# Taking the sign into the slope of an activation while 64-bit weights are decoded, and a new emission order

## The chip, the cores and the metric

The kernel runs on one core of a Trainium2 chip. The metric is device time in microseconds of one execution, the median of several. The engines are named as in the profile: PE (TensorE), DVE (VectorE), ACT (ScalarE), POOL (GpSimd) and SP (SyncE, which here issues nearly all DMAs). Each runs its own queue in order, and they wait for each other by semaphores.

## The reference, cut to what matters

An mLSTM layer over 4 batches, 8 heads, 768 steps and 40 channels, then a gated feed-forward layer over the 3072 tokens of 320 channels.

```python
for t in range(S):
    m_new = np.maximum(f_gate[:, :, t] + m, i_gate[:, :, t])
    f_stab, i_stab = np.exp(f_gate[:, :, t] + m - m_new), np.exp(i_gate[:, :, t] - m_new)
    C = f_stab * C + i_stab * outer(v_t, k_t);  n = f_stab * n + i_stab * k_t
    y[:, :, t] = sigmoid(o_gate[:, :, t]) * (C @ q_t) / np.maximum(np.abs(n . q_t), 1.0)
x = y.transpose(0, 2, 1, 3).reshape(B * S, H * D)
out = (sigmoid(x @ w_gate) * (x @ w_val)) @ w_out
```

The three weights (320x1536 twice, 1536x320) arrive as 64-bit floats. No engine computes on those, so the kernel reads them as pairs of 32-bit words and makes the 32-bit float out of the bits.

## The kernel before, in words

The 768 steps are cut into 6 chunks of 128. A chunk c and a batch b make a *unit* u = 4c + b (8 heads of 128 steps), 24 units in all. A unit goes through stages: `a` transposes q and k and lays q out block-diagonally; `e` (`dmat`) makes the matrix of decays, an exponential and a mask; `b` makes the scores and multiplies them with the decays; `c` multiplies with v, adds what comes from the state, divides by the denominator (`halfden`, `times_den`), updates the state and issues the loads of the same batch's next chunk; `d` transposes the result into the feed-forward layer's input (`xh`, `xl`, a high and a low part, since PE's fast format holds fewer bits).

The feed-forward layer of a chunk has 12 steps j over the hidden channels. A *tile* is one step for some batches: (c, j, 0, 4) for all four, or two half tiles (c, j, 0, 2) and (c, j, 2, 4). PARAM['K'] says how many steps of a chunk are halved; for chunk 0 it is 4, so its tiles 0 to 7 are halves: tiles 0 to 3 for batches 0 and 1, tiles 4 to 7 for batches 2 and 3. Tiles 8 to 15 of chunk 0 are whole. `ffn_up` makes gate and value on PE (L496 to L501), a tanh on ACT (L503), the product on DVE (L504), the high part on ACT (L507) and the low part on DVE (L508). `ffn_down` adds to the four outputs (L518 to L520).

The weights are decoded on the way, all during chunk 0. There are 30 decodings, numbered in `wseq`: for each i of 6, gate rows, value rows, the rest rows of both, and two blocks of w_out. One decoding (`w_dec`) is: the absolute value of the high word on ACT (L242, into one of three buffers `dc`); a clamp (L247) and a mask with shift by 3 bits (L248) on DVE; an OR of the sign and the top bit of the exponent (L252) and an OR of the low word's top 3 bits (L253) on DVE; the high part on ACT (L278, L281 or L283); the low part on POOL (L288, L292 or L294), with which the buffer is free. `w_more` then issues the load of a later weight block on SP into the staging tile that came free.

The opening handles units 0 and 1 and decodings 0 to 2 in an order given by PARAM['open'] (names such as `wvb`: weight, value, stage b; `kw0`: k times the last decays, unit 0). All else is emitted in the order of PARAM['pos'], where position n is n whole tiles of feed-forward work after its start; a half tile takes half a position. In the text "before tile n" counts the tiles above, while positions count whole ones. Positions are first pushed to where the data need them. A down-projection of the tile before comes at PARAM['down'] of a tile. Work below PARAM['pin'] is held behind the opening on each engine, and `opening_end` (the states of units 0 and 1) comes at PARAM['ce']. The emission order decides the queues' order but for priorities: decodings have a raised one (WPO), stages too (HPO).

Of the kernel before, what the change touches and what calls it, by code (L numbers as in the profile page):

```python
# [9 lines left out]
F32 = mybir.dt.float32  # L10
F32R = mybir.dt.float32r
I32 = mybir.dt.int32
AF = mybir.ActivationFunctionType
ALU = mybir.AluOpType

EXP_LOW = struct.unpack("<f", struct.pack("<I", 0x38000000))[0]
EXP_HIGH = struct.unpack("<f", struct.pack("<I", 0x47EFFE00))[0]


PARAM = {  # L20
    'pos': {
# [15 lines left out]
    },  # L37
    'V32': 1,
    'HPO': 1,
    'WPO': 10,  # L40
    'TS': False,
    'down': 0.6,
    'K': [4, 12, 3, 0, 0, 12],
    'eng': {
# [3 lines left out]
    },  # L48
    'warm': 6,
    'pin': 2,  # L50
    'ce': -9,
    'open': {
# [8 lines left out]
        'wvc': 59.0, 'wvd': 60.0, 'na1': 69.87, 'xt0': 62.0, 'wve': 63.0, 'wrb': 64.0, 'nb1': 62.99, 'wrc': 61.877,  # L61
        'xt1': 56.016, 'wrd': 70.043, 'wre': 69.0, 'kw1': 70.0, 'e2': 87.0,
    },
    'unpin': [],
}
# [4 lines left out]
def mlstm_then_gated_ffn_kernel(  # L70
# [13 lines left out]
    nc = tc.nc  # L84
# [139 lines left out]
    wh, wl, w2 = [], [], []  # L224
# [14 lines left out]
    def decode_abs(st, n):  # L239
        dc = stage.tile([P, 2 * FW], F32, tag="dc", name=f"dc_{n}", bufs=3)  # L240
        t = dc[:, : st.shape[1]]
        nc.scalar.activation(t, st[:, :, 1].bitcast(F32), AF.Abs)  # L242
        return t

    def decode_exp(st, t):
        ti = t.bitcast(I32)
        nc.vector.tensor_scalar(t, t, EXP_LOW, EXP_HIGH, ALU.max, ALU.min)  # L247
        nc.vector.tensor_scalar(ti, ti, 0x07FFFFFF, 3, ALU.bitwise_and, ALU.logical_shift_left)  # L248

    def decode_bits(st, t):  # L250
        ti = t.bitcast(I32)
        nc.vector.scalar_tensor_tensor(ti, st[:, :, 1], -0x40000000, ti, ALU.bitwise_and, ALU.bitwise_or)  # L252
        nc.vector.scalar_tensor_tensor(ti, st[:, :, 0], 29, ti, ALU.logical_shift_right, ALU.bitwise_or)  # L253

    wq = {}
# [40 lines left out]
    def w_dec(part, i):  # L296
        st = w_stage(part, i)
        t = decode_abs(st, f"{part}_{i}")
        decode_exp(st, t)
        decode_bits(st, t)  # L300
        w_high(part, i, t)
        w_low(part, i, t)
# [235 lines left out]
    def opening():  # L538
# [130 lines left out]
        def w_a(x):  # L669
            w[x] = decode_abs(w_stage(*x), "%d_%d" % x)  # L670

        def w_b(x):
            decode_exp(w_stage(*x), w[x])

        def w_c(x):
            decode_bits(w_stage(*x), w[x])
# [169 lines left out]
    ce = PARAM["ce"]  # L846
    for p, (kind, kk) in events:
        if ce is not None and p >= ce:
            pinned(opening_end)
            ce = None  # L850
# [33 lines left out]
```

## Time and profile before

| | |
|---|---|
| median of 3 runs | 612.86 us (609.75 to 613.76) |
| the profiled execution | 612.63 us, span 610.9 us, mean granted clock 0.963 |
| busy in the span | PE 93%, DVE 65%, ACT 38%, POOL 36% |
| instructions | 9801 |
| moved by DMA | 43.91 MB, mean 72 GB/s |

The span runs from the first to the last instruction; the execution's time has some more around it. Busy times are of one execution. A row of a group gives line, engine, operation, output and inputs, count, busy us and mean ns; a row of the timeline gives start, duration, engine, line, and in brackets the idle time before it and what ended it; a row of stretches gives start:end, length, then busy time and count of PE, PEld (weight loads), DVE, ACT and POOL, the granted clock of PE as a share of full speed, the DMA share and GB/s.

### The profile page before, as it was taken

How to read it: one execution, taken by the hardware profiler on the slowest of the kernel's cores; microseconds unless marked ns; L12 is line 12 of the kernel's file. 1: busy time of each engine (PE TensorE's matmuls, PEld its weight loads, DVE VectorE, ACT ScalarE, POOL GpSimd, SP SyncE). 2: the span in 40 equal slices, each digit the busy share in tenths (PEclk: the TensorE clock that was granted, in tenths of full speed). 3: DMA queues.
4: the chain of work that ended last, by engine and by line, in shares of the span. 5: the costliest groups of instructions: out<-in, count | busy, mean ns of one | idle time of the engine just before them, and what ended most of it. 6: DMA issues, size and time to landing. Idle time of an engine off the chain costs nothing.

```text
span 610.9 us, 9801 instructions
## 1 busy us (share of the span) xinstructions
PE 566.9 (93%) x3601; PEld 511.4 (84%) x3601; DVE 396.4 (65%) x822; ACT 234.1 (38%) x580; POOL 221.6 (36%) x277
## 2 busy tenths in 40 slices
PE   8568898898999999999989999989999999999997
PEld 7456787676999899898878888879788888999997
DVE  5798889997454887846676647566656566533332
ACT  5274557535343334442332252332242322132322
POOL 5466355955142464524343324432322321100000
PEclk9766899998999999999999999998899999999999
DMA  9774665413132224413032232131232200010000
GB/s 194 227 180 130 128 187 147 125 33 88 45 78 68 73 50 115 92 28 79 12 77 58 56 76 64 25 77 37 43 79 54 57 1 0 1 45 1 23 1 21
DMA packets 112847, 43.91 MB, mean 72 GB/s; under 512 B 101280, under 2 KB 104544, under 8 KB 112800
## 3 DMA queue, kind: packets, MB, share of 16 engines
q1 hardware_dynamic: 111712, 43.04, 28.6%
q8 instruction: 28, 0.46, 0.3%
q10 hardware_dynamic: 1088, 0.26, 0.2%
q14 instruction: 19, 0.16, 0.1%
HBM read 39.26 MB, written 4.03 MB: 71 GB/s over the span
## 4 chain that ended last, share of the span: by engine, by line
PE 63%; DVE 20%; DMA 4%; ACT 3%; issue 3%; SPq 3%; POOL 3%; DVEq 0%; POOLq 0%; ACTq 0%
PE pg L496 25%; PE po L520 5%; PE po L519 5%; PE po L518 5%; PE av L416 5%; PE pg L498 4%; PE pg L501 4%; DVE bh L369 3%; PE s L400 3%; DVE gl L508 3%; PE in L411 2%; DVE dc L253 2%; DVE kl L362 2%; DVE dc L252 2%; DVE sg L504 1%
## 5 line engine op out<-in xcount | busy, mean ns | idle before, releaser
L496 PE MATMUL pg<-xh,wh 128*128 128x256 f32 (+1 forms) x412 | 118.9, 353 | 3.3 <-ACT sg L503 1.6
L504 DVE SCALAR_TENSOR_TENSOR sg<-sg,pg 128x256 f32<-128x256 f32 (+1 forms) x103 | 53.9, 523 | 100.5 <-ACT sg L503 93.7
L503 ACT ACTIVATE sg<-pg 128x256 f32<-128x256 f32 (+1 forms) x103 | 48.3, 469 | 182.7 <-PE pg L501 178.4
L496 PE MATMUL pg<-xh,wl 128*128 128x256 f32 (+1 forms) x412 | 113.9, 343 | 0.0
L496 PE MATMUL pg<-xl,wh 128*128 128x256 f32 (+1 forms) x412 | 110.1, 336 | 0.0
L520 PE MATMUL po<-oh,gl 128*128 128x320 f32 x288 | 97.1, 339 | 1.9 <-DVE gl L508 1.9
L519 PE MATMUL po<-ol,gh 128*128 128x320 f32 x288 | 97.1, 337 | 0.0
L518 PE MATMUL po<-oh,gh 128*128 128x320 f32 x288 | 94.9, 329 | 0.4 <-ACT gh L507 0.4
L508 DVE TENSOR_TENSOR gl<-sg,gh 128x256 fp32r<-128x256 f32 (+1 forms) x103 | 69.2, 672 | 30.4 <-ACT gh L507 29.2
L496 PEld LDWEIGHTS pg<-xh,wh 128*128 128x128 f32 x412 | 72.7, 194 | 10.9 <-DVE sg L504 2.7
L496 PEld LDWEIGHTS pg<-xh,wl 128*128 128x128 f32 x412 | 72.1, 195 | 6.5
L496 PEld LDWEIGHTS pg<-xl,wh 128*128 128x128 f32 x412 | 71.8, 194 | 6.5
L369 POOL TENSOR_TENSOR bl<-kl,bmask 120x384 fp32r<-120x384 f32 (+1 forms) x48 | 49.3, 1032 | 58.2 <-DVE kl L362 56.1
L507 ACT ACTIVATE gh<-sg 128x256 fp32r<-128x256 f32 (+1 forms) x103 | 51.6, 501 | 48.4 <-DVE sg L504 48.1
L520 PEld LDWEIGHTS po<-oh,gl 128*128 128x128 f32 x288 | 54.8, 191 | 4.3 <-DVE gl L508 4.0
L518 PEld LDWEIGHTS po<-oh,gh 128*128 128x128 f32 x288 | 55.5, 193 | 3.0 <-ACT gh L507 0.6
L519 PEld LDWEIGHTS po<-ol,gh 128*128 128x128 f32 x288 | 55.2, 191 | 0.8
L416 PEld LDWEIGHTS av<-v,d 128*128 128x128 f32 x352 | 52.0, 191 | 3.3 <-DVE d L393 2.2
L498 PE MATMUL pg<-xh,w 128*128 128x256 f32 (+1 forms) x206 | 53.5, 336 | 0.0
L501 PE MATMUL pg<-xl,w 128*128 128x256 f32 (+1 forms) x206 | 52.7, 333 | 0.0
L416 PE MATMUL av<-v,d 128*128 128x41 f32 x352 | 49.9, 254 | 2.1 <-DVE d L393 1.6
L218 POOL TENSOR_SCALAR_AFFINE_SELECT d<-d 128x1024 f32<-128x1024 f32 x22 | 26.8, 1220 | 66.2 <-ACT d L213 61.5
(132 smaller groups left out, 977.9 us busy)
## 6 DMA issues: line engine op xcount, KB each, us to landing
d<-mscr SPq DMA_DIRECT2D x22, 512.0 KB, 3.8
k<-in_k_dram SPq DMA_DIRECT2D x24, 160.0 KB, 3.4
v<-in_v_dram SPq DMA_DIRECT2D x24, 160.0 KB, 3.7
o<-in_o_gate_dram SPq DMA_DIRECT2D x24, 160.0 KB, 3.4
st_o<-in_moe_w_out_dram SPq DMA_DIRECT2D x12, 320.0 KB, 2.9
out_dram<-ob SPq DMA_DIRECT2D x24, 160.0 KB, 1.8
q<-in_q_dram SPq DMA_DIRECT2D x23, 160.0 KB, 2.9
st<-in_moe_w_gate_dram SPq DMA_DIRECT2D x6, 512.0 KB, 3.7
```

The costliest lines, as they stand in the source:

```text
L369: eng.tensor_tensor(dst[:r, g, :nh, :], src[:r, g, 0, :].bitcast(F32).unsqueeze(1).broadcast_to([r, nh, L]), bmask[:r, :nh, :], ALU.mult)
L416: nc.tensor.matmul(pv[:, h, :], dm[u][:, h, :], vt[u][:, h, :], start=True, stop=True)
L496: nc.tensor.matmul(pg[n], w[n][:, a, fs], x[c][:, a, n0:n1], start=(i + a == 0), stop=False)
L498: nc.tensor.matmul(pg[n], w2[n][:, fs], xh[c][:, 2, n0:n1], start=False, stop=False)
L501: nc.tensor.matmul(pg[n], w2[n][:, fs], xl[c][:, 2, n0:n1], start=False, stop=True)
L503: nc.scalar.activation(sg, pg[0], AF.Tanh, scale=0.5)
L504: nc.vector.scalar_tensor_tensor(sg, sg, 1.0, pg[1], ALU.add, ALU.mult)
L507: last = nc.scalar.activation(gh[u][:, :nt], sg, AF.Copy)
L508: E('gl0' if c == 0 else 'gl').tensor_tensor(gl[u][:, :nt], sg, gh[u][:, :nt].bitcast(F32), ALU.subtract)
L518: nc.tensor.matmul(po[t], g1[:, ts], oh[:, j, :], start=(j == 0), stop=False)
L519: nc.tensor.matmul(po[t], g1[:, ts], ol[:, j, :], start=False, stop=False)
L520: nc.tensor.matmul(po[t], g0[:, ts], oh[:, j, :], start=False, stop=(j == NF - 1))
```

## The change

The absolute value on ACT becomes a leaky slope: f(x) = x for x >= 0, alpha * x for x < 0, on x times 2^-112, with alpha = 2^32. A positive number comes out scaled by 2^-112, a negative one by 2^-80. The difference of 32 in the exponent puts the sign where the shift by 3 bits brings it to the top, with the exponent's top bit right for both signs. So the clamp gets other bounds, the mask before the shift goes, and the OR of the sign (L252) goes. The tiles, buffers and engines of what is left are the same.

Besides, nearly all positions of PARAM['pos'] and PARAM['open'] are new, with `down` 0.6 to 0.66, `pin` 2 to 4.6, `ce` -9 to -8.79.

```diff
-EXP_LOW = struct.unpack("<f", struct.pack("<I", 0x38000000))[0]
-EXP_HIGH = struct.unpack("<f", struct.pack("<I", 0x47EFFE00))[0]
+MAX_POS = struct.unpack("<f", struct.pack("<I", 0x0FEFFFFF))[0]
+MAX_NEG = struct.unpack("<f", struct.pack("<I", 0x9FEFFFFF))[0]
...
-    'down': 0.6,
+    'down': 0.66,
...
-    'pin': 2,
-    'ce': -9,
+    'pin': 4.6,
+    'ce': -8.79,
...
-        nc.scalar.activation(t, st[:, :, 1].bitcast(F32), AF.Abs)
+        nc.scalar.activation(t, st[:, :, 1].bitcast(F32), AF.Prelu, scale=2.0**-112, alpha=2.0**32)
...
-        nc.vector.tensor_scalar(t, t, EXP_LOW, EXP_HIGH, ALU.max, ALU.min)
-        nc.vector.tensor_scalar(ti, ti, 0x07FFFFFF, 3, ALU.bitwise_and, ALU.logical_shift_left)
+        nc.vector.tensor_scalar(t, t, MAX_POS, MAX_NEG, ALU.min, ALU.max)
+        nc.vector.tensor_scalar(ti, ti, 3, None, ALU.logical_shift_left)
...
-        nc.vector.scalar_tensor_tensor(ti, st[:, :, 1], -0x40000000, ti, ALU.bitwise_and, ALU.bitwise_or)
         nc.vector.scalar_tensor_tensor(ti, st[:, :, 0], 29, ti, ALU.logical_shift_right, ALU.bitwise_or)
```

Of the new positions, those of chunk 0 that stand elsewhere in the sorted order (p before -> after, in whole tiles):

| event | before | after |
|---|---|---|
| stages b, c, d of unit 2 | 1.01, 1.30, 1.42 | 0.70 |
| stages a, b, c, d of unit 3 | 1.01, 1.30, 1.30, 1.60 | 0.70 |
| first down-projection | 0.80 (at 0.6 of a tile of 0.5, from 0.5) | 0.83 |
| stages a, b, d of unit 4 | 2.18, 4.53, 5.50 | 1.79, 3.89, 7.62 |
| decodings 19; 20 to 22; 23; 24, 25 | 7.38; 7.99; 8.99; 9.99 | 7.38; 7.42; 7.44; 7.45 |
| decodings 26, 27 | 9.99 | 9.99 |
| stage e of units 7, 8 | 9.99, 12.73 | 11.32, 16.27 |

Later units see stage e moved by up to 1.7 later or 1.1 earlier, stages a and b by up to 2.1 earlier, stage c of the third batch by 1 later, and stage d of unit 10 by 2.2 later. In the opening `kw0` goes from behind `dl0` to behind `wvb`.

More of the change, by code (lines that the diff above doesn't have):

```diff
@@ L49 @@
     'warm': 6,
-    'pin': 2,
-    'ce': -9,
+    'pin': 4.6,
+    'ce': -8.79,
     'open': {
[8 rows of a table removed]
-        'wvc': 59.0, 'wvd': 60.0, 'na1': 69.87, 'xt0': 62.0, 'wve': 63.0, 'wrb': 64.0, 'nb1': 62.99, 'wrc': 61.877,
-        'xt1': 56.016, 'wrd': 70.043, 'wre': 69.0, 'kw1': 70.0, 'e2': 87.0,
[9 rows of a table added]
+        62.625, 'wve': 63.0, 'wrb': 63.947, 'nb1': 61.739, 'wrc': 61.877, 'xt1': 57.363, 'wrd': 70.043, 'wre': 69.0,
+        'kw1': 70.796, 'e2': 87.005,
     },
```

47 rows, old and new, of the table PARAM are left out of this document.

## The prediction, made before the result was known

> **What bounds the kernel now.** I read the shares of the engines first, then the busy time by stretches, then the cadence of the feed-forward tiles, then the chain that ended last.
>
> ```profile
> PE 566.9 (93%) x3601; PEld 511.4 (84%) x3601; DVE 396.4 (65%) x822; ACT 234.1 (38%) x580; POOL 221.6 (36%) x277
> ...
> 0.00:30.00 30.00, 20.96 (x114) 17.95 (x114) 18.91 (x41) 12.21 (x34) 14.42 (x35) 0.89 0.87 213
> 30.00:55.00 25.00, 17.01 (x71) 13.33 (x71) 24.97 (x61) 15.84 (x49) 17.55 (x17) 0.57 0.60 148
> 55.00:75.00 20.00, 18.14 (x113) 15.92 (x113) 15.18 (x37) 10.86 (x34) 8.50 (x13) 0.85 0.58 137
> 75.00:150.00 75.00, 66.17 (x370) 55.97 (x370) 68.32 (x125) 42.82 (x106) 48.18 (x47) 0.98 0.44 121
> 150.00:611.00 461.00, 444.61 (x2941) 408.23 (x2939) 269.05 (x562) 152.36 (x360) 132.91 (x168) 0.99 0.20 48
> ```
>
> Over the whole span TensorE is the bound, but the average hides two regimes. In the rows of the stretches (PE, PEld, DVE, ACT, POOL, then the granted clock) PE is busy 96% after 150 us and DVE only 58%. Between 30 and 55 us DVE is busy 24.97 of 25.00 us while PE has 17.01 at a granted clock of 0.57; between 75 and 150 us DVE has 91% and PE 88%. So VectorE sets the pace up to 150 us, TensorE after it. How much is to be had there? One tanh (L503) stands in each feed-forward tile:
>
> ```profile
> 39.10 0.38 ACT L503 ACTIVATE sg<-pg 128x256 f32<-128x256 f32 x1
> ...
> 77.70 0.38 ACT L503 ACTIVATE sg<-pg 128x256 f32<-128x256 f32 x1 [1.88 <-PE pg L501]
> ...
> 118.49 0.60 ACT L503 ACTIVATE sg<-pg 128x512 f32<-128x512 f32 x1
> 126.04 0.60 ACT L503 ACTIVATE sg<-pg 128x512 f32<-128x512 f32 x1 [2.12 <-PE pg L501]
> 138.10 0.60 ACT L503 ACTIVATE sg<-pg 128x512 f32<-128x512 f32 x1
> ...
> 156.08 0.38 ACT L503 ACTIVATE sg<-pg 128x256 f32<-128x256 f32 x1 [2.14 <-PE pg L501]
> ```
>
> The first chunk of 12 tiles runs from 39.10 to 156.08, 117.0 us; the other five share 610.9 - 156.1 = 454.8 us, 91.0 each. The first is 26 us slower, and 39.10 to 77.70 alone (two tiles, 38.6 us where 2 x 7.6 is the later pace) accounts for 23 of them. That is the room for any change to the decoding.
>
> **The removed OR.** L252 is the sign's OR, L253 the other one, which stays. The first two rows give min/median/max in ns; the next four are the busy time of L252 alone, by the same stretches.
>
> ```profile
> L252 DVE SCALAR_TENSOR_TENSOR dc<-st,dc x18: 410/683/1382, 6.7 to 134.8; 128x512 int32<-128x512 int32 x12, 128x256 int32<-128x256 int32 x6
> L252 DVE SCALAR_TENSOR_TENSOR dc<-st_o,dc x12: 472/482/2069, 37.4 to 146.3; 128x320 int32<-128x320 int32 x12
> ...
> 0.00:30.00 30.00, 1.79 (x3) 0.89 0.87 213
> 30.00:55.00 25.00, 4.11 (x6) 0.57 0.60 148
> 55.00:75.00 20.00, 1.16 (x2) 0.85 0.58 137
> 75.00:150.00 75.00, 15.47 (x19) 0.98 0.44 121
> ```
>
> Thirty instructions go: 22.5 us measured. Their unstretched price is 12 x 0.683 + 6 x 0.410 + 12 x 0.480 = 16.4 us. The difference of 6 us is waiting, and this is what such a wait looks like:
>
> ```profile
> 46.95 1.88 POOL L218 TENSOR_SCALAR_AFFINE_SELECT d<-d 128x1024 f32<-128x1024 f32 x1
> 47.19 0.68 DVE L252 SCALAR_TENSOR_TENSOR dc<-st,dc 128x512 int32<-128x512 int32 x1
> ...
> 47.99 1.38 DVE L253 SCALAR_TENSOR_TENSOR dc<-st,dc 128x512 int32<-128x512 int32 x1
> 49.29 0.28 DVE L247 TENSOR_SCALAR dc<-dc 128x256 f32<-128x256 f32 x1
> ```
>
> L253 takes twice its median while POOL's mask of 1.88 us runs, yet the L252 just before it is not stretched, so the stretch isn't strict. I expect it to pass to the next instruction when one is removed, and count 16.4; 22.5 stays as the upper end. The Trainium skill ("SBUF — State Buffer", section "SBUF: two separate sides") says more: GpSimd and a VectorE instruction with two SBUF inputs take a port pair by exclusive lock. By that rule the whole excess would move on, as I count it; the unstretched row at 47.19 does not agree with it.
>
> Stretch by stretch:
>
> *0 to 30 us.* Only the third OR stands before something that PE waits for:
>
> ```profile
> 25.08 0.42 DVE L252 SCALAR_TENSOR_TENSOR dc<-st,dc 128x256 int32<-128x256 int32 x1
> 25.54 0.42 DVE L253 SCALAR_TENSOR_TENSOR dc<-st,dc 128x256 int32<-128x256 int32 x1
> 25.89 0.16 DVE L431 TENSOR_SCALAR den<-av 128x8 f32<-128x8 f32 x1
> ...
> 27.78 1.20 PE L452 MATMUL xt<-ident,x 128*128 128x128 f32 x3 [4.62 <-POOL x L441]
> ```
>
> The denominator of the second unit stands behind it, POOL's product behind that, PE's transposition last. Start to start the OR takes 25.54 - 25.08 = 0.46 us: I count 0.4. The other two (1.4 us) lie beside the waits for PE and ACT: nothing.
>
> *30 to 75 us.* DVE never rests until 55, so all six ORs there are on the path: unstretched 3 x 0.48 + 2 x 0.683 + 0.41 = 3.2. Of the two after it (1.16), half: 0.6. Bounds 2.2 (what of them the chain holds, below) and 5.3.
>
> *75 to 150 us.* Nineteen ORs, 15.5 us measured, unstretched 8 x 0.48 + 7 x 0.683 + 4 x 0.41 = 10.3. The chain gives the lower end:
>
> ```profile
> by line: DMA v<-in_v_dram 16.9%; DMA q<-in_q_dram 12.7%; DVE dc L252 9.5%; PE pg L496 8.2%; DVE dc L253 8.2%; issue 7.2%; DVE gl L508 4.6%; DVE qbd L346 4.1%; DVE gin L168 3.1%; ACT d L209 3.1%; PE po L520 3.0%; PE s L392 2.8%; DVE dc L247
> by line: DVE gl L508 10.5%; PE av L416 9.9%; DVE dc L253 9.8%; DVE dc L247 7.5%; issue 7.0%; PE pg L496 6.9%; POOL ol L294 5.1%; DVE d L393 4.8%; DVE sg L504 4.3%; PE cs L464 3.6%; DVE dc L252 3.4%; PE xt L452 3.4%; ACT gh L507 2.9%; PE po
> by line: DVE dc L252 8.5%; issue 8.1%; PE pg L496 6.2%; DVE dc L253 6.0%; POOL wl L288 5.6%; POOL qbd L346 5.2%; POOL ol L294 4.9%; DMA st_o<-in_moe_w_out_dram 4.4%; ACT d L209 3.9%; POOL d L218 3.5%; DVE sg L504 3.3%; DVE dc L248 3.0%; POO
> ```
>
> These are 30 to 60, 60 to 100 and 100 to 160 us. L252 holds 9.5% of 30, 3.4% of 40 and 8.5% of 60 us: 2.9 + 1.4 + 5.1 = 9.3 us, or 6.8 at 16.4/22.5. Some 6.5 of the 9.3 lie after 60 us; unstretched (10.3/15.5) that is 4.3. The upper end is PE's idle time in the stretch, 75 - 66.17 = 8.8, as PE has its work to do whatever DVE does. I take 5, near the chain.
>
> Sum: 0.4 + 3.2 + 0.6 + 5 = 9.2 us. After 150 us no decoding is left, and PE at 96% goes on as before: nothing.
>
> **What takes the OR's place.** ScalarE's absolute value becomes a sloped one with the same tiles, one for one. No row shows it; the nearest rows are those it replaces and the copies of the same size, so 0 is taken, between -0.1 and +0.1 us each. ACT is 54 to 63% busy in the stretches of decoding, which covers +0.1 x 30 = 3 us. If that cover were gone, the 3 us would come off the 9.2. The clamp keeps its two operations, the shift loses one of two in the same instruction: nothing.
>
> ```profile
> L242 ACT ACTIVATE dc<-st x18: 430/666/702, 5.1 to 131.2; 128x512 f32<-128x512 f32 x12, 128x256 f32<-128x256 f32 x6
> L242 ACT ACTIVATE dc<-st_o x12: 477/491/504, 33.3 to 143.7; 128x320 f32<-128x320 f32 x12
> L555 ACT ACT_TABLE_LOAD x1 | 1.3, 1283 | 1.8 <-PEq L869 1.8
> ```
>
> **The new order.** Sorted by position, the two lists differ in three moves that could matter. (1) In the opening kw0 goes behind the value weights' clamp: one POOL product of 128x320, as the one here, for which POOL has 1.23 us of idle time just before it: nothing.
>
> ```profile
> 18.32 0.72 POOL L441 TENSOR_TENSOR x<-o,den 128x320 f32<-128x320 f32 x1 [1.23 <-DVE o L435]
> ```
>
> (2) The stages b, c, d of units 2 and 3 were emitted behind tile 2, the last of them behind tile 3; now they all come ahead of the first down-projection and of tiles 2 and 3. The loads that stage c issues on SP pass nothing, as no weight load is emitted between the old places and the new. Tile 4 needs unit 3, so it may gain the DVE work of two tiles, 2 x (0.41 + 0.97) = 2.8 us. It may lose PE's filler, about 2.1 us a half tile:
>
> ```profile
> 54.17 0.80 PE L496 MATMUL pg<-xh,wh 128*128 128x256 f32 x2
> ...
> 54.66 0.41 DVE L504 SCALAR_TENSOR_TENSOR sg<-sg,pg 128x256 f32<-128x256 f32 x1
> ...
> 55.59 0.97 DVE L508 TENSOR_TENSOR gl<-sg,gh 128x256 fp32r<-128x256 f32 x1
> ...
> 56.05 1.05 PE L392 MATMUL s<-qbd,qk 80*128 80x256 f32 x2
> ```
>
> Behind units 2 and 3 wait then tiles 2 and 3 in PE's queue, and ACT and DVE for them: up to 2 x 2.1 = 4.2 us. Between -2.8 and +4.2 I take 0. (3) Decodings 20 to 25 move up by a half to two and a half tiles, so that seven come in one run with 19; the loads that they issue pass those of one unit on SP, which is needed tiles later. The work is the same at another time: 0, unless it jams (below). The rest, masks and exponentials of later units emitted later, moves inside a stretch in which PE is busy 96%: 0, between -2 and +2.
>
> Forecast: span 610.9 - 9.2 = 601.7 us. The profiled execution took 612.63, 1.7 more than its span and 0.2 under the median of 612.86, so **603.4 us**. Its own range: at best 0.4 + 5.3 + 8.8 + 2.8 + 2 = 19.3 less, 593; at worst 6.8 less and 4.2 + 2 more, 612.
>
> **Rivals.** *POOL takes over.* Its L288, L346, L294 and L218 hold 5.6 + 5.2 + 4.9 + 3.5 = 19.2% of the chain from 100 to 160 us, 11.5 us, and three kinds of ACT's waits between 30 and 160 us are for it (us, times, longest):
>
> ```profile
> ACT dc L242 <- POOL ol L294: 4.7, 4, 2.1
> ...
> ACT dc L242 <- POOL wl L288: 2.4, 3, 1.1
> ...
> ACT dc L242 <- POOL w L292: 1.2, 1, 1.2
> ```
>
> The decoding has three buffers, and a new one begins when POOL has made the low part of an old one. If POOL paces the decoding after 75 us, the 5 us are lost: 612.6 - 4.2 = 608. Against it: POOL is busy 48 of 75 us there.
>
> *A jam, slower than before.* Four decodings in one run (24 to 27, emitted before tile 14) already stretch one tile: 126.04 to 138.10 is 12.1 us, against 7.55 from 118.49, so +4.5 for four. Place: ACT and POOL between tiles 11 and 13; ACT's tanh stands behind absolute values that wait for buffers. If the cost grows with the square, seven cost 4.5 x 49/16 = 13.8, less 4.5 no longer paid: +9.3. With the gain up to 75 us (4.2) it is 612.6 + 5.1 = 618. It decides from the point where more than three buffers are asked for before POOL returns one.
>
> *The slope isn't in the loaded table, so the change doesn't do what it says.* One load of 1.28 us stands in the trace. If each decoding needed one and the next exp or tanh another, 27 decodings after 30 us cost 27 x 2.57 = 69 us of ACT, whose busy time from 30 to 150 us is 69.5 us: 139 for 120 us, at least +19 less 9 of gain: 622. The Trainium skill ("ScalarE: Activation LUTs", section "Table sets: the hidden batching unit") lists exp, tanh, relu and abs in one set and does not name the parametric one; no run here shows it yet.
>
> *More than forecast.* PE at 0.57 of its clock until 55 us could stay warm if DVE feeds it: 17.01 x 0.43 = 7 us more, 596 or less.
>
> **How the numbers follow.** Forecast 0.62; POOL 0.25; jam 0.07; table 0.03; more 0.03. A measurement here tells 1% (6 us) from nothing: faster is below 606.7. Of the forecast 0.56 lies there, of POOL's case 0.05, all of "more": 0.64. Slower is jam and table, 0.10; the rest 0.26. The range leaves out the jam, the table and the edges: 593 to 612.
>
> **What would show it.** No L252-like OR; DVE at 374 to 380 us (396.4 less 22.5 to 16.4); the first chunk near 108 us by the tanh rows, the others still 91; one table load; the sloped activation at 0.67 us for 512. I am wrong if DVE drops by 20 us and the chunk doesn't shorten (POOL or PE late next), if an interval near tile 12 exceeds 15 us (jam), or if chunks after the first change by over 2 us in all (then the order counts, which I priced at nothing).

## The result, and the profile after

The changed kernel takes 590.85 us (median of 4 runs, 588.73 to 593.32) against 613.12 us for the kernel before, a ratio of 0.9649 with a 95% interval of [0.9596, 0.9702]. (The ratios, here and below, are worked out from the single runs and are not the quotients of the medians.) One run of e11 (772.75 us) and one of the kernel before beside e1 (1364.24 us) were slow and are left out of all that follows. The forecast was 603.4, with a range from 593 to 612: the direction was right, the size was not, and the time lies below the range. The profiled execution took 590.19 us, span 588.5, so 22.4 us of span went, where 9.2 were forecast.

The page of the kernel after, busy time of the engines and then the same stretches as before (start:end, length, PE, PEld, DVE, ACT, POOL, granted clock, DMA share, GB/s):

```profile
PE 557.1 (95%) x3601; PEld 507.1 (86%) x3601; DVE 373.5 (63%) x792; ACT 233.4 (40%) x580; POOL 213.7 (36%) x277
...
0.00:30.00 30.00, 21.09 (x116) 17.84 (x116) 17.25 (x41) 14.28 (x41) 16.06 (x36) 0.87 0.90 216
30.00:55.00 25.00, 18.55 (x95) 15.73 (x95) 20.54 (x56) 15.78 (x47) 16.63 (x20) 0.61 0.73 183
55.00:75.00 20.00, 17.94 (x133) 16.39 (x133) 16.99 (x39) 13.58 (x41) 11.80 (x16) 1.00 0.80 198
75.00:150.00 75.00, 70.94 (x417) 61.69 (x415) 57.10 (x108) 42.04 (x104) 36.41 (x40) 1.00 0.38 102
150.00:589.00 439.00, 428.56 (x2848) 395.44 (x2846) 261.57 (x549) 147.71 (x349) 132.84 (x167) 1.00 0.21 48
```

VectorE lost 22.9 us of work, where the removed OR had 22.5, and between 30 and 55 us it is busy 20.54 us where it was 24.97 of 25. Two rows say more than that: from 55 us on TensorE has its full clock (0.85 and 0.98 in those two stretches before), and the last stretch, where nothing is decoded, is 97.6% busy after 96.4%. The rows of the feed-forward tanh (L503 before, L506 after) show where the time went:

```profile
42.63 0.36 ACT L506 ACTIVATE sg<-pg 128x256 f32<-128x256 f32 x1
...
70.52 0.39 ACT L506 ACTIVATE sg<-pg 128x256 f32<-128x256 f32 x1 [1.62 <-DVE gl L511]
...
142.23 0.36 ACT L506 ACTIVATE sg<-pg 128x256 f32<-128x256 f32 x1
```

The first tile comes 3.5 us later (39.10 to 42.63; just before it TensorE waits 3.88 us in one piece for VectorE's copy `qk`, L346, and why that comes so late stays open), yet tile 4 comes 7.2 us earlier (77.70 to 70.52) and chunk 1 begins 13.9 us earlier (156.08 to 142.23). The rest, 8.5 us, comes after chunk 0: chunks 2 and 3 get shorter by 3.3 and 6.6 us, as the table below shows. So there are two questions: why chunk 0 gained more than the OR's price, and why chunks gained in which nothing is decoded.

The replaced instructions, by tile and by line (min/median/max in ns; busy us, mean ns):

```profile
L246 ACT ACTIVATE dc<-st x18: 425/662/722, 5.1 to 114.6; 128x512 f32<-128x512 f32 x12, 128x256 f32<-128x256 f32 x6
L246 ACT ACTIVATE dc<-st_o x12: 481/494/509, 31.1 to 122.1; 128x320 f32<-128x320 f32 x12
L558 ACT ACT_TABLE_LOAD x1 | 1.3, 1283 | 1.8 <-PEq L872 1.8
L252 DVE TENSOR_SCALAR dc<-dc x30: 281/408/1793, 6.3 to 124.3; 128x512 int32<-128x512 int32 x12, 128x320 int32<-128x320 int32 x12, 128x256 int32<-128x256 int32 x6
```

The slope costs what the absolute value did (medians of 666 and 491 ns before), and one table load serves the kernel. (L252 is now the shift, not the OR.)

### The profile page after: what moved, and what is told of

Its sections match the earlier page's. It is cut to its first block, busy times and chain, and to the rows that moved or that the text cites. A ratio compares the mean times of both kernels' runs of the same rounds, so it can differ in the third digit from the quotient of the medians.

```text
span 588.5 us, 9783 instructions
## 1 busy us (share of the span) xinstructions
PE 557.1 (95%) x3601; PEld 507.1 (86%) x3601; DVE 373.5 (63%) x792; ACT 233.4 (40%) x580; POOL 213.7 (36%) x277
## 4 chain that ended last, share of the span: by engine, by line
PE 77%; DVE 12%; ACT 5%; issue 2%; DMA 2%; POOL 1%; POOLq 0%; DVEq 0%; ACTq 0%
PE pg L499 30%; PE po L523 6%; PE po L522 6%; PE po L521 6%; PE av L419 5%; PE pg L501 5%; PE pg L504 5%; PE s L403 4%; PE in L414 2%; DVE gl L511 2%; DVE bh L372 2%; PE cs L467 2%; DMA o<-in_o_gate_dram 1%; PE pt L363 1%; PE xt L455 1%
## 5 line engine op out<-in xcount | busy, mean ns | idle before, releaser
L499 PE MATMUL pg<-xh,wh 128*128 128x256 f32 (+1 forms) x412 | 115.4, 348 | 2.1 <-ACT sg L506 1.6
L506 ACT ACTIVATE sg<-pg 128x256 f32<-128x256 f32 (+1 forms) x103 | 48.2, 468 | 173.5 <-PE pg L504 164.5
L499 PE MATMUL pg<-xh,wl 128*128 128x256 f32 (+1 forms) x412 | 112.6, 343 | 0.0
L499 PE MATMUL pg<-xl,wh 128*128 128x256 f32 (+1 forms) x412 | 107.5, 335 | 0.0
L522 PE MATMUL po<-ol,gh 128*128 128x320 f32 x288 | 97.6, 339 | 0.0
L523 PE MATMUL po<-oh,gl 128*128 128x320 f32 x288 | 95.0, 330 | 1.1 <-DVE gl L511 1.1
L499 PEld LDWEIGHTS pg<-xh,wh 128*128 128x128 f32 x412 | 71.1, 192 | 7.8 <-ACT sg L506 2.7
L419 PEld LDWEIGHTS av<-v,d 128*128 128x128 f32 x352 | 52.7, 192 | 1.5 <-PE in L414 0.9
L419 PE MATMUL av<-v,d 128*128 128x41 f32 x352 | 50.5, 254 | 0.8 <-issue 0.8
L372 DVE TENSOR_TENSOR bh<-kh,bmask 120x384 fp32r<-120x384 f32 (+1 forms) x48 | 44.3, 923 | 0.0
```

The costliest lines, as they stand in the source:

```text
L372: eng.tensor_tensor(dst[:r, g, :nh, :], src[:r, g, 0, :].bitcast(F32).unsqueeze(1).broadcast_to([r, nh, L]), bmask[:r, :nh, :], ALU.mult)
L419: nc.tensor.matmul(pv[:, h, :], dm[u][:, h, :], vt[u][:, h, :], start=True, stop=True)
L499: nc.tensor.matmul(pg[n], w[n][:, a, fs], x[c][:, a, n0:n1], start=(i + a == 0), stop=False)
L506: nc.scalar.activation(sg, pg[0], AF.Tanh, scale=0.5)
L522: nc.tensor.matmul(po[t], g1[:, ts], ol[:, j, :], start=False, stop=False)
L523: nc.tensor.matmul(po[t], g0[:, ts], oh[:, j, :], start=False, stop=(j == NF - 1))
```

## The experiments

All times of this table are of one profiled execution each, read from the tanh rows: when the first tile, tile 4 and chunk 1 come, how long chunks 1, 2 and 3 take, and the span. The median is over several executions. "u23" stands for the five new positions a2, c2, d2, b3, d3, which place units 2 and 3; the other names are those of the runs.

| run | first | tile 4 | chunk 1 at | 1 | 2 | 3 | span | median |
|---|---|---|---|---|---|---|---|---|
| before | 39.1 | 77.7 | 156.1 | 107.4 | 94.9 | 96.1 | 610.9 | 613.12 |
| after | 42.6 | 70.5 | 142.2 | 108.3 | 91.6 | 89.5 | 588.5 | 590.85 |
| e1: slope, old order | 44.4 | 79.9 | 156.6 | 107.8 | 94.9 | 93.8 | 609.6 | 610.03 |
| e2: new order, OR kept | 38.6 | 77.0 | 153.9 | 104.8 | 91.6 | 89.5 | 597.8 | 599.28 |
| e3: before + 7 late positions | 39.0 | 77.0 | 155.6 | 108.5 | 90.9 | 89.5 | 603.0 | 606.63 |
| e4: after, those 7 put back | 41.1 | 69.0 | 140.6 | 104.5 | 97.6 | 93.5 | 592.8 | 600.98 |
| e5: slope + u23 | 43.7 | 70.6 | 145.3 | 108.4 | 94.9 | 93.5 | 598.6 | 602.19 |
| e6: after, u23 put back | 41.2 | 72.2 | 149.1 | 104.3 | 91.6 | 89.5 | 592.9 | 594.45 |
| e7: after, decodings put back | 44.2 | 72.1 | 144.0 | 105.4 | 91.6 | 89.8 | 588.4 | 590.39 |
| e8: after, opening put back | 44.5 | 72.7 | 144.4 | 106.9 | 91.7 | 89.5 | 590.5 | 590.87 |
| e9: before + es3, cs2 | 37.9 | 76.4 | 155.4 | 107.0 | 94.8 | 92.6 | 606.9 | 609.05 |
| e10: before, state addition on POOL | 41.0 | 79.5 | 158.1 | 106.2 | 93.6 | 91.4 | 605.9 | 608.41 |
| e11: slope + u23 + es3, cs2 | 42.0 | 68.8 | 143.3 | 107.9 | 94.0 | 91.8 | 594.1 | 595.92 |
| e12: after, decodings and opening put back | 44.1 | 72.0 | 143.9 | 104.6 | 91.6 | 89.8 | 587.7 | 589.12 |
| e13: before + as2 | 39.9 | 78.0 | 157.5 | 107.8 | 93.8 | 91.0 | 606.9 | 608.64 |
| e14: before + as2, cs2 | 39.2 | 77.7 | 156.9 | 106.3 | 91.8 | 89.0 | 600.3 | 603.78 |
| e15: slope + u23 + as2, cs2 | 43.7 | 70.3 | 145.0 | 112.4 | 91.8 | 89.0 | 594.1 | 592.23 |

Profiled executions differ: in e4 the profiled one took 594.70 us, 6.3 less than its median, in e15 595.82, 3.6 more. So verdicts go by the ratios, each against runs of the kernel before beside it, and the table tells where to look.

### Slope or order: e1 and e2

e1 is the kernel before with the decoding's lines of the diff (the slope in, the OR out) and the old order; e2 keeps the old decoding, OR and all, and takes the new order.

> The new decoding under the old emission order. Theory A (two causes that add: the removed instruction shortens the first chunk, the order of the later units takes the waits out of chunks 2 and 3): the first chunk ends 7 to 14 us earlier, chunks after it unchanged, 600 to 606 us. Theory B (the order does nearly all): 609 to 613 us. Theory C (the decoding does nearly all, and the 8.6 us after the first chunk are a dip of the clock that happens to go): 588 to 594 us.

> The old decoding with the OR of the sign, under the new emission order. Theory A: chunks 2 and 3 shorter by 8 to 10 us, first chunk by 0 to 4, 599 to 605 us. Theory B: 589 to 595 us. Theory C: 610 to 614 us. If the order needs the shorter decoding in the first chunk, the first chunk gets longer than before and the total stays above 605.

e1: 610.03 us, ratio 0.993 [0.9887, 0.9972], as its theory B had it. e2: 599.28 us, ratio 0.9754 [0.9695, 0.9813], as its theory A had it. The slope is worth 0.7% by itself, the order alone 2.5%, most of it after chunk 0.

In chunk 0 neither does much alone: chunk 1 begins 0.6 us later in e1, 2.2 us earlier in e2, and 13.9 us earlier with both. Up to chunk 1 the two do not add; some 12 us need both. These are single profiled executions, but they repeat well: the four runs with the old chunk 0 (e3, e9, e13, e14) begin chunk 1 between 155.4 and 157.5 us, the three with the slope and u23 (e5, e11, e15) between 143.3 and 145.3. In the time of the whole execution it does not show: 0.7% and 2.5% make 3.2%, and both together are worth 3.5% [3.0%, 4.0%]. The stretch of e2 between 30 and 55 us goes with the order doing little there by itself:

```profile
30.00:55.00 25.00, 16.33 (x69) 13.45 (x70) 24.96 (x59) 15.34 (x47) 17.35 (x18) 0.64 0.63 152
```

With the OR, DVE is busy 24.96 of 25 us in the new order and 24.97 in the old. In e1 DVE has room, and TensorE does not get the use of it for long: tile 3 comes 3.3 us earlier than in the kernel before (68.25 to 64.92), tile 4 then 2.2 us later. The stretches of e1, first 30 to 55 us, then 5 us each, and its timeline:

```profile
30.00:55.00 25.00, 15.69 (x88) 13.27 (x87) 20.68 (x56) 16.89 (x52) 15.51 (x18) 0.75 0.69 171
...
55.00:60.00 5.00, 4.64 (x35) 3.88 (x33) 4.07 (x8) 2.49 (x6) 2.91 (x3) 1.00 0.61 145
60.00:65.00 5.00, 3.54 (x26) 2.92 (x25) 5.00 (x12) 4.33 (x16) 3.47 (x4) 1.00 0.65 189
65.00:70.00 5.00, 4.30 (x18) 3.89 (x18) 2.64 (x7) 1.85 (x6) 2.68 (x4) 0.64 0.81 187
70.00:75.00 5.00, 4.59 (x21) 4.23 (x22) 2.59 (x10) 2.04 (x8) 0.39 (x3) 0.50 0.34 58
75.00:80.00 5.00, 4.78 (x22) 4.34 (x21) 1.62 (x3) 1.94 (x6) 3.40 (x4) 0.50 0.67 210
```

```profile
58.39 1.98 PE L419 MATMUL av<-v,d 128*128 128x41 f32 x16 [0.36 <-DVE qk L346]
...
62.73 0.81 PE L395 MATMUL s<-qbd,qk 120*128 120x384 f32 x2
65.69 0.56 PE L395 MATMUL s<-qbd,qk 120*128 120x384 f32 x1 [2.16 <-DVE d L396]
...
67.54 3.47 PE L419 MATMUL av<-v,d 128*128 128x41 f32 x16
```

DVE's row is full from 60 to 65 us. At the head of TensorE's queue stand unit 3's scores, and they wait 2.16 us for DVE's product that takes up the earlier ones (L396). On DVE it stands behind the product with the denominator (L444) and the OR of a decoding's low word (L256):

```profile
62.93 1.55 DVE L444 TENSOR_TENSOR x<-o,den 128x320 f32<-128x320 f32 x1
64.40 0.68 DVE L256 SCALAR_TENSOR_TENSOR dc<-st,dc 128x512 int32<-128x512 int32 x1
65.00 0.55 DVE L396 TENSOR_TENSOR d<-s,d 128x384 f32<-128x384 f32 x1
```

Behind that wait the granted clock is 0.64, 0.50 and 0.50, and 16 products (L419) of a shape that took 1.98 us at 58.39 now take 3.47. TensorE looks busy (4.30 to 4.78 of 5) with 18 to 22 products in each stretch, where it had 35 in the first. Later in e1 two more waits of 2.08 and 3.00 us, ending at 121.93 and 127.64 us, come with a clock of 0.78 and 0.87 between 125 and 135 us.

### Which part of the order chunk 0 needs: e5 to e8 and e12

```diff
 e5: before + slope, and (e6: after with the reverse)
-'a2': -1.609, 'c2':  5.73,  'd2': 1.423, 'b3': 3.931, 'd3': 1.597
+'a2': -1.889, 'c2': 16.422, 'd2': 0.76,  'b3': 6.705, 'd3': 0.7
 e7: after, every position of a decoding (w2, w3, w5 ... w29) as before
 e8: after, 'open', 'pin' and 'ce' as before
 e12: e7 and e8 in one
```

> The kernel before with the new decoding and, of the new order, only the positions of units 2 and 3 (a2, c2, d2, b3, d3), so that their stages come ahead of the first down-projection. The decoding alone left the first tanh of tile 4 at 79.9 us and that of chunk 1 at 156.6. Theory A (the order of units 2 and 3 and the decoding need each other): tile 4 at 69 to 73 us, chunk 1 at 144 to 150, 600 to 604 us. Theory B (the places of the decodings decide): tile 4 at 77 to 80, 608 to 611 us. Theory C (the opening's order decides): the same as B.

> The changed kernel with the positions of units 2 and 3 put back. Theory A: tile 4 at 76 to 80 us, chunk 1 at 148 to 156, 597 to 604 us. Theories B and C: as the changed kernel, tile 4 at 70 to 71 us, 589 to 593 us.

> The changed kernel with the positions of all decodings put back. Theory A: within 2 us of the changed kernel, chunk 1 at 141 to 145 us, 589 to 594. Theory B: chunk 1 at 148 us or later, 597 to 604 us. The jam of the prediction: the interval of tanhs near tile 11 and 12 (7.9 and 8.9 us in the changed kernel) gets shorter.

> The changed kernel with the opening's order, ce and pin put back. Theories A and B: tile 4 within 2 us of 70.5, 589 to 594 us. Theory C: tile 4 at 75 to 80 us, 596 to 604 us.

> The changed kernel with the positions of all decodings and the opening (order, ce, pin) put back at once, as neither alone cost anything: 587 to 593 us if they count for nothing together, and a version at least as fast with less changed; over 595 us if one covers for the other.

e5: 602.19 us, ratio 0.9834 [0.9781, 0.9887]. Five positions bring chunk 1 from 156.6 to 145.3 us when the slope is in. The stretches of e5, to be read against those of e1:

```profile
65.00:70.00 5.00, 3.99 (x31) 3.50 (x30) 3.93 (x10) 4.36 (x15) 3.53 (x5) 1.00 0.92 152
70.00:75.00 5.00, 4.79 (x37) 4.53 (x37) 3.67 (x7) 3.01 (x9) 4.69 (x6) 1.00 1.01 274
75.00:80.00 5.00, 5.00 (x42) 5.00 (x41) 1.75 (x4) 1.68 (x5) 1.21 (x2) 1.00 0.76 209
```

With units 2 and 3 ahead of tiles 2 and 3, the 2.16 us wait is gone and the clock stays at 1.00. Between 65 and 80 us e1 was short of 5 x (0.36 + 0.50 + 0.50) = 6.8 us of full clock; with the wait of 2.16 that is 9.0 us, and tile 4 comes 9.25 us earlier in e5 (79.89 to 70.64). The sum is of the size of the difference, but no proof: the two orders do other work before tile 4, and tiles 2 and 3 come 4.5 and 2.6 us later in e5. That the wait is what lowered the clock is inferred from their order in time, and the length of a wait alone does not decide it, as e6 shows next. No run moves these five positions with the OR kept and all else as before.

e6: 594.45 us, ratio 0.9703 [0.9656, 0.975]. Chunk 1 begins at 149.1 us, as theory A had it, but the time lies below its 597 to 604 us and tile 4 comes at 72.2 us, not at 76 to 80. The stretches of e6, and its wait for the same product:

```profile
55.00:75.00 20.00, 16.79 (x118) 14.42 (x119) 16.82 (x38) 12.31 (x38) 13.15 (x17) 1.00 0.74 198
75.00:150.00 75.00, 68.02 (x376) 57.63 (x375) 55.51 (x101) 40.11 (x101) 34.74 (x39) 0.95 0.36 92
...
PE s L395 <- DVE d L396: 1.6, 1, 1.6
```

Units 2 and 3 stand at their old places here and the wait is still there, with 1.59 us; the clock stays at 1.00, and tile 4 is nearly as early as in the kernel after. So in this order the old places cost no more than 1.7 us up to tile 4; the fallen clock is what e1 has and e6 has not. As the two differ in the rest of the order too, that is a strong hint and no proof. e6 loses its time later: TensorE waits 3.60 us, up to 115.31 us, for a tanh, and the clock is 0.68 and 0.64 in the next two stretches of 5 us. So u23 is one way of spending the freed time, not the only one. The intervals of e6 and of the whole change overlap.

e7: 590.39 us, 0.9627 [0.9595, 0.966]; e8: 590.87 us, 0.9621 [0.9587, 0.9654]; e12: 589.12 us, 0.9625 [0.9565, 0.9685]. None can be told from the whole change. (Tile 4 of e8 comes 2.2 us later, just outside of what was expected, and in e7 the intervals from tiles 11 and 12, 9.0 us each, did not get shorter.) The run of seven decodings and the new opening, some two thirds of the diff's new numbers, make no difference that can be measured.

### The later chunks: e3, e4, e9, e10, e13, e14

The seven late positions (as0, bs0, es1, as2, cs2, bs3, es3) place the units from chunk 2 on.

```diff
 e3: before + (e4: after with the reverse)
-'as0': 1.974, 'bs0': 5.746, 'es1': -0.646, 'as2': 6.565, 'cs2': 8.091, 'bs3': 9.884, 'es3': 5.632
+'as0': 1.416, 'bs0': 9.682, 'es1': 1.067, 'as2': 4.504, 'cs2': 9.123, 'bs3': 9.636, 'es3': 6.155
 e9: before + es3, cs2     e13: before + as2     e14: before + as2, cs2
 e10: before, and
-'ca': 'v'
+'ca': 'p'
```

> The kernel before, with only the seven changed positions of units 12 and later (as0, bs0, es1, as2, cs2, bs3, es3). Theory A: the additions to the state at 316, 408 and 428 us no longer wait 2.1 us, chunks 2 and 3 are 8 to 10 us shorter and nothing else moves: 603 to 605 us. Theory C: 611 to 614 us.

> The changed kernel with those seven positions put back. Theory A: the first chunk as in the changed kernel (99.6 us from its first tanh), chunks 2 and 3 as before the change, 597 to 601 us. Theory C: 590 to 592 us.

e3: 606.63 us, ratio 0.9883 [0.9808, 0.9958], a little over the 603 to 605 of theory A; e4: 600.98 us, 0.9759 [0.9681, 0.9837]. These seven are worth 7 us added to the kernel before and about as much (0.9759 against 0.9649, intervals that just overlap) taken from the one after. What they take away stands in the kernel before in its timeline, and in its waits of TensorE in chunks 2 and 3 (us in total, times, longest):

```profile
315.31 2.22 POOL L212 TENSOR_TENSOR d<-at,d 128x1024 f32<-128x1024 f32 x1
...
315.69 2.10 DVE L481 TENSOR_TENSOR cst<-cst,ct 120x246 f32<-120x246 f32 x1
317.72 0.41 DVE L362 TENSOR_TENSOR kl<-pt,kh 120x256 fp32r<-120x256 f32 x1
318.05 0.28 DVE L367 COPY qk<-pt 120x128 f32<-120x128 f32 x1
...
318.48 0.30 PE L452 MATMUL xt<-ident,x 128*128 128x128 f32 x1 [2.08 <-DVE qk L367]
...
PE xt L452 <- DVE qk L367: 4.1, 2, 2.1
```

DVE's addition to the state (L481) takes 2.10 us while POOL subtracts two arrays (L212); the other single additions of this shape take 0.38 to 0.43 us. The row of the line has the median over both shapes:

```profile
L481 DVE TENSOR_TENSOR cst<-cst,ct x32: 227/402/2105, 105.0 to 449.9; 120x246 f32<-120x246 f32 x16, 80x82 f32<-80x82 f32 x16
```

DVE's copy of the next unit's transposition (L367) stands behind the addition. TensorE's transposition L452 takes a PSUM bank of the same pool as `pt`, and waits for the copy. The Trainium skill ("SBUF — State Buffer", section "SBUF: two separate sides") says that a VectorE instruction with two SBUF inputs and a GpSimd one that reads SBUF exclude each other for a whole instruction; the 2.10 beside the 2.22 us agree with it. Three single additions are stretched like that, at 315.69, 408.38 and 428.10 us. (Two rows of two additions are as well, at 351.92 and 448.03 us, with no long wait behind them.) What follows differs. Behind the first TensorE waits 2.08 us and its clock stays at 1.00; behind the second it waits 2.07 us and the clock falls; behind the third it has other work, then waits 0.87 and 0.53 us at 434 and 436 us, and the clock falls too. The stretches of chunks 2 and 3 in the kernel before, and of chunk 3 in e14:

```profile
263.00:358.00 95.00, 91.14 (x569) 81.31 (x568) 59.92 (x120) 32.26 (x76) 34.25 (x44) 1.00 0.24 54
358.00:454.00 96.00, 92.21 (x522) 80.27 (x521) 60.55 (x114) 31.30 (x70) 33.57 (x42) 0.96 0.24 57
408.00:418.00 10.00, 7.93 (x37) 6.93 (x36) 8.16 (x14) 2.65 (x7) 4.94 (x5) 0.83 0.30 52
428.00:438.00 10.00, 8.59 (x41) 6.67 (x40) 8.14 (x14) 2.19 (x6) 4.81 (x4) 0.93 0.34 60
```

```profile
355.00:444.00 89.00, 88.72 (x522) 78.16 (x521) 58.24 (x114) 31.26 (x70) 34.22 (x42) 1.00 0.27 61
```

The same 522 records of TensorE take 96 us in the one, and 89 in the other with the clock at 1.00.

> The kernel before with two positions changed, es3 (the decays of every fourth unit, 5.632 to 6.155) and cs2 (8.091 to 9.123). Theory A (in chunks 2 and 3 a state addition on DVE starts just behind POOL's subtraction for the decays and stands for 2.1 us, which makes PE wait and lose its clock): no addition over 1.2 us is left, chunks 2 and 3 from 94.9 and 96.1 to 91 and 89.5 us, 604 to 607 us. Theory B (the other five late positions do it): 611 to 614 us.

> The kernel before with the state's additions on POOL in place of DVE: nothing on DVE can then stand there behind POOL's subtraction. Theory A: PE's waits for qk copies in chunks 2 and 3 shrink, these chunks get 3 to 8 us shorter, 604 to 610 us, unless POOL's own queue (36% busy before) gets late with the masks. Theory B: chunks 2 and 3 as before, 611 to 616 us.

My first guess at the positions was wrong. e9 took 609.05 us, 0.9947 [0.9909, 0.9986], and its waits still hold both long ones in chunks 2 and 3:

```profile
PE xt L452 <- DVE qk L367: 4.1, 2, 2.1
```

Only the addition at 428 us has moved: it is still stretched (two additions in 2.04 us at 433.79 us), but no wait of over 1 us comes of it, and chunk 3 takes 92.6 us for 96.1. By e14 below, which leaves es3 out, that was cs2. e10 leaves the order alone and takes the addition off DVE: 608.41 us, 0.9921 [0.9883, 0.996], chunk 3 shorter by 4.7 us and no wait longer than 0.9 us in chunks 2 and 3. No position moved in e10, so the waits hang on the addition standing on DVE, not on something else in the order.

> The kernel before with one position changed: as2 from 6.565 to 4.504, so that stage a of the third unit of each chunk is no longer given out right behind a state update on VectorE. Theory A (the 2.1 us state additions at 315 and 408 us come from where stage a of the next unit stands, and cost only because TensorE's transposes wait for the copy of qk behind them): no such wait of about 2.1 us at 315 and 408, chunk 2 from 94.9 to 91 to 92 us, chunk 3 from 96.1 to 92 to 93 us (the one at 428 us stays), 606 to 609 us. Rival (the collision is a matter of when GpSimd's subtraction falls, which this position does not move): both waits stay, 611 to 614 us.

> The kernel before with as2 from 6.565 to 4.504 and cs2 as in the new order. Theory A (these two of the seven late positions carry the late gain): as with all seven, chunk 2 at 91 us, chunk 3 at 89.5 us, 604 to 608 us. Rival (it takes more of the seven): chunk 2 stays at 94 to 95 us, chunk 3 at 93 to 94 us, 609 to 612 us.

e13: 608.64 us, 0.992 [0.9881, 0.9958]. One position, as2, removes the waits at 315 and 408 us; two stretched additions are still there (at 334.31 and 425.32 us, 2.11 and 2.10 us), with nothing longer than 0.9 us of TensorE behind them. Chunk 2 came to 93.8 us, over the expected 91 to 92, chunk 3 to 91.0, under the expected 92 to 93; so which of them costs how much was only roughly right. e14: 603.78 us, 0.986 [0.983, 0.989]: a little under the 604 to 608 expected; with cs2 no wait of over 1 us is left, and chunks 2 and 3 are as in the kernel after. This is how two additions, merged in one row, look in e14 when they fall into POOL's subtraction (DVE, then POOL):

```profile
316.27 2.34 DVE L481 TENSOR_TENSOR cst<-cst,ct 120x246 f32<-120x246 f32 x2 [1.69 <-ACT ct L476]
...
316.61 1.90 POOL L212 TENSOR_TENSOR d<-at,d 128x1024 f32<-128x1024 f32 x1 [1.07 <-DMA d<-mscr]
```

The copies of the next unit have been made before, and so TensorE does not wait behind them: the stretch is still there, what stood behind it has gone. Two positions out of all carry the gain of the later chunks, as far as the intervals can tell.

### Both together: e11 and e15

```diff
 before + slope + u23, and
+ e11: 'es3', 'cs2' as after
+ e15: 'as2', 'cs2' as after
```

> The kernel before with the new decoding and only seven new positions: the five of units 2 and 3, es3 and cs2. If these are what counts: chunk 1 starts at 144 to 147 us, chunks 2 and 3 at 91 to 92 and 89 to 90 us, 593 to 597 us. If the rest of the order matters as much: 599 to 603 us.

> The kernel before with the slope and seven positions: a2, c2, d2, b3, d3 of the first chunk's units 2 and 3, and as2 and cs2 of the later ones. Theory A (the slope needs units 2 and 3 moved; as2 and cs2 remove the collisions; nothing else of the change counts): chunk 1 starts at 143 to 146 us, chunks 2 and 3 take 91 to 92 and 89 to 90 us, 589 to 594 us, as the whole change. Rival (other positions carry part of it): 597 us or more, with chunk 2 or 3 at 94 us or more.

e11, made while es3 was still my guess, took 595.92 us, 0.9746 [0.9667, 0.9825], and kept its stretched additions in chunks 2 and 3 (303.49 and 395.3 us), with 94.0 and 91.8 us for these chunks, not the 91 to 92 and 89 to 90 of its expectation. e15 took 592.23 us, 0.9678 [0.9639, 0.9717], which can't be told from the whole change. By the ratios e5 gave 10.2 us and e14 8.6, together 18.8; e15 gave 19.7. Within the intervals the two causes add. Its chunk 1 of 112.4 us belongs to the profiled execution, the slowest of its four, with the clock at 0.83 in 15 us of that chunk.

No version was clearly better than the kernel after: e12 and e7 are nearest, and their intervals overlap its own.

## Why the prediction was wrong, by its own steps

- **What bounds the kernel: right up to 55 us and after 150, too simple between.** The change freed 4.4 us of DVE between 30 and 55 us. In e1 DVE is busy 53.50 of the 75 us from 75 to 150, 71% after 91%, and the way from tile 4 to chunk 1 got only 1.6 us shorter (78.4 to 76.8).
- **"0.4 + 3.2 + 0.6 + 5 = 9.2 us": the sum was made as if freed VectorE time were time won.** In the old order that was wrong: alone it is worth 0.7% [0.3%, 1.1%], 1.7 to 6.9 us (e1), and nothing up to the beginning of chunk 1 in the profile. The forecast did not ask what TensorE would do next: it had unit 3's scores at the head of its queue, 2.16 us of wait, and a clock that fell. In the new order the same step (e2 to the kernel after) takes the span from 597.8 to 588.5 us, the forecast's 9.2 almost to the digit (by the ratios 1.05%, some 6.4 us). It is 11.6 us up to chunk 1 less 2.3 after it, so that so close a hit is in part luck. What the forecast lacked in all is the 13.1 us of span (2.5% by the ratio) that the order brings in e2, priced at 0 in the next two steps.
- **"Between -2.8 and +4.2 I take 0" for units 2 and 3: this step failed, in size and by its bounds.** With the slope the move is worth 0.993 less 0.9834, 5.9 us by the ratios, and 11.3 us at the beginning of chunk 1 by the profiles. I bounded it by the DVE work of two tiles and by TensorE's filler, in the old state of the queue, where DVE was full and the whole order brought only 2.2 us up to chunk 1 (e2). It had to be priced together with the OR. Tiles 2 and 3 did come later, as I feared (by 4.5 and 2.6 us in e5 against e1), but tile 4 came 9.25 us earlier.
- **"The rest ... moves inside a stretch in which PE is busy 96%: 0, between -2 and +2": this failed too.** as2 and cs2 alone are worth 1.4% [1.1%, 1.7%], 8.6 us (e14). A share of 96% over 461 us leaves 16.4 us idle, and the few long waits among them were named in the waits of the kernel before. I read the average and not those rows. The text did say that a change of over 2 us in the later chunks would mean that the order counts.
- **The moved decodings and the opening at 0: right** (e7, e8, e12). The *jam* did not come: the longest interval of tanhs after tile 4 is 9.5 us in the kernel after, where it was 12.1. A wait of its kind is what e6 loses by: the tanh at 114.68 us there stands on ACT behind an absolute value that waited 1.52 us for a buffer from POOL.
- **The slope's price, the single table load, POOL not next: right.** The sloped activation took a median of 662 ns against 666 (twelve of 512 and six of 256), L558 is the only table load, and POOL is busy 36.41 of 75 us between 75 and 150 us.
- **DVE at 374 to 380 us: 373.5.** The shift, costed at no change for one operation less, got no cheaper: 30 of them took 15.7 us (mean 537 ns) where they had taken 12.7 (433). Where it is not stretched it costs the same (0.41 to 0.43 us of 512 in both), so the 3.0 us are waiting; "I expect it to pass to the next instruction" came true for that part.
- **"More than forecast", the clock: a rival that was in part right and had too small a chance (0.03).** Between 30 and 55 us the clock rose from 0.57 to 0.61 only, in e1 to 0.75, where it bought nothing in the end; between 55 and 75 us it rose from 0.85 to 1.00. How much of the gain is the clock's own no run separates.

## What to carry to other kernels

Where an engine is full, price the removal of its work and a new order together: with DVE full the order brought 2.2 us up to chunk 1, with the old order the freed time brought nothing there, and both at once gave 13.9 us up to chunk 1 (in the time of the whole execution the intervals here are too wide to tell that from a sum). Then ask, for the stretch where the bound goes away, what stands at the head of the next engine's queue. In a stretch that looks saturated on average, go through the list of waits for the few of 2 us: behind some of them the clock falls as well, and a single position can remove them.

## What was not expected of the hardware

- A wait of TensorE of only 2.16 us was followed by some 15 us at a granted clock of 0.50 to 0.64 (e1, 65 to 80 us) although TensorE's row was busy 86 to 96% by then. In the kernel before, a wait of 2.07 us was followed by 0.83 over 10 us (408 to 418 us) and one of 1.21 us, ending at 69.05 us, by 0.66 over 5 us (70 to 75 us). But behind 2.08 us at 318 us and 1.59 us in e6 the clock stayed at 1.00, so what decides it stays open. The Trainium skill ("TensorE: Matmul & The Clock Gate", section "What's actually happening") puts the fall behind an idle window of about 3.4 us; in e1 the clock is at 1.00 from 55 to 65 us, and that wait of 2.16 us is the only one of over 0.4 us in the ten before the fall, so that less idle time than that was enough here.
- A state addition on VectorE went from 0.38 to 0.43 us to 2.10 us beside GpSimd's subtraction of two arrays of 2.22 us.
- The shift by itself was not cheaper than mask and shift in one instruction. Its median rose from 327 to 408 ns because more of them were stretched; unstretched it is the same. The row of the kernel before, by line, to be read against L252 of the kernel after:

```profile
L248 DVE TENSOR_SCALAR dc<-dc x30: 277/327/1162, 6.3 to 145.9; 128x512 int32<-128x512 int32 x12, 128x320 int32<-128x320 int32 x12, 128x256 int32<-128x256 int32 x6
```
